# The gate row is spread over the partitions by GpSimd, with two short fillers among TensorE's first transposes

## The chip, the cores and the metric

The kernel runs on one core of a Trainium2 chip. The metric is the device time of one execution in microseconds. A core has five engines that run their own instruction streams in order: TensorE (PE, with its weight loads shown apart as PEld), VectorE (DVE), ScalarE (ACT), GpSimd (POOL) and SyncE (SP, here a queue for DMAs only). They meet through semaphores. PE writes to PSUM (eight banks of 512 fp32 columns), the others work on SBUF, and both memories have 128 partitions.

## The reference

Two branches work on the same x (2048 positions by 512), and a gate mixes them:

```
x = A_x
g = _sigmoid((x * gate_w).sum(-1, keepdims=True))
a = _A_ref(x, A_wqkv, A_wo)
b = _B_ref(x, B_w1, B_b1, B_w2, B_b2)
return g * a + (1 - g) * b
```

Branch a is a local attention: 32 heads of 16, each position attends to 8 positions at distances 0, 2, ... 14, then a product with `wo`. Branch b normalises each row of x, multiplies along the positions with w1 (2048 by 1792), adds b1, takes gelu, and multiplies back with w2, plus b2. The change concerns `gate_w`: the gate's sum for each position needs the 512 numbers of `gate_w` in every partition, since positions lie on the partitions.

## The kernel before

x is held as 16 tiles of 128 positions by 512 (`X`). PE's stream runs in this order: five products on constants (`f_warm`, line 568), transposes of the first four tiles of x (`tx`, line 586) mixed with the first part of branch b on the first four normalised tiles (`lead`, line 618), then the q, k and v projections (line 713), the first product of branch b (`f_ph2`, line 609), in which the two sums of the attention's logits are put (`f_sum`, line 803, called sum0 and sum1), and at the end, tile by tile, the second product of branch b (`f_ph3`, line 937) and the product with `wo` (`f_wo`, line 946). The element-wise products of the attention (q times the shifted k, their sums `qadd`, weights times v) all run on DVE as `tensor_tensor` through the helper of line 468, for two halves of the positions; GpSimd starts DMAs that add or spread parts of them (lines 831, 880, 901).

The program writes each operation with an estimated duration, what it reads and writes, a priority and, in `after`, operations that must have been started. A planner (`_Sched`) runs a list schedule over these estimates when the program is built and so fixes each engine's order; PE's own order is a chain written by hand (`PE`). At run time the order is kept, and an engine waits on the semaphores of what an operation needs. So an operation that comes later than the planner estimated holds up whatever stands behind it on its engine.

The opening, which the change touches, goes like this. For each of the first four tiles t, DVE takes statistics (`stat`, line 623, and `aggr`, line 627), ScalarE makes the reciprocal deviation in two small steps (`rstd`), and DVE normalises the tile (`apply`, line 634) for `lead(t)`. PE transposes the raw tile (`tx(t)`) and an engine copies it from PSUM to `XT` (`ext`, line 598 or 599), which the projections read. The transposed tiles lie in banks 4, 5, 5 and 7 (`TXB`), the transposed biases (`f_tb`, lines 602 and 603) in bank 7; small DVE copies (lines 674 and 675) take them out. The first projections use banks 4 to 7 in turn; those of k on the first 512 positions are called pjk0 to pjk3.

The gate row: ScalarE's queue loads `gate_w` into one partition (line 533) of a tile `GWZ` that GpSimd has set to zero (line 478). A product with a matrix of ones (line 643, `gwbc`) sums over the partitions, so each row of bank 6 holds `gate_w`, and ScalarE copies it to `GWB` (line 656, `evgw`). DVE's 16 gate sums (line 756, z0 to z15) read it. z0 to z5 stand at the head of DVE's stream behind the last normalisation; `rp` (line 679) makes a small indicator matrix for the sums of line 803, and the first q times k product (line 816) follows. GpSimd writes the identity for the transposes (`IDENT`, line 475) right behind two memsets.

Of the kernel before, what the change touches and what calls it, by code (L numbers as in the profile page):

```python
# [5 lines left out]
BF16 = mybir.dt.bfloat16  # L6
# [3 lines left out]
AF = mybir.ActivationFunctionType  # L10
# [3 lines left out]
D = 512  # L14
# [4 lines left out]
NST = S // 128  # L19
NFT = F // 128  # L20
# [8 lines left out]
NLEAD = 4  # L29
AVD = (1, 3, 5, 6)  # L30
GL = 4
# [259 lines left out]
class _Mem:  # L291
# [17 lines left out]
    def view(self, name, dtype, dims, extra=0, p0=0, np_=128):  # L309
        base = self.arena[:].bitcast(dtype)  # L310
        pst = base.ap[0][0]
        esz = mybir.dt.size(dtype)
        o = self.off[name]
        assert o % esz == 0
        return bass.AP(base.tensor, p0 * pst + o // esz + extra, [[pst, np_]] + [list(d) for d in dims])


def bass_gated_mix__sliding_local_dilated__mixer_token_mlp__prompt_kernel(nc, A_x, A_wqkv, A_wo, B_x, B_w1, B_b1, B_w2, B_b2, gate_w, out, dbg=None):
    with contextlib.ExitStack() as es:
# [35 lines left out]
        view = m.view  # L355

        def psub(ap_, p0, np_, offs, dims):
            pst = ap_.ap[0][0]
            return bass.AP(ap_.tensor, ap_.offset + p0 * pst + offs, [[pst, np_]] + [list(d) for d in dims])

        ps = es.enter_context(nc.psum_tensor("ps", [128, 8, 512], FP32))
        esem = {e: es.enter_context(nc.semaphore("sem_" + e)) for e in ("pool", "act", "dve", "pe")}
        sch = _Sched()
        A = sch.add
# [33 lines left out]
        LOG = [view("LOG", BF16, [(UT_, NW), (1, UT_)], extra=h * NW * UT_) for h in range(2)]  # L398
# [12 lines left out]
        E32 = view("E32", FP32, [(1, D)])  # L411
        GWB = view("GWB", BF16, [(1, D)])
        LX = view("LX", BF16, [(D, NLEAD), (1, D)])
        GWZ = view("LOG", BF16, [(1, D)], extra=NLEAD * 128 * GL)
        GW1 = psub(GWZ, 0, 1, 0, [(1, D)])
        JUNK = view("S4", BF16, [(D, 4), (1, D)])
        ZN = view("Z", FP32, [(1, 32)])
        TZ = view("Z", FP32, [(1, 32)], extra=32)
# [2 lines left out]
        IDENT = view("IDENT", BF16, [(1, 128)])  # L421
# [4 lines left out]
        B1R = view("ROWS", BF16, [(1, 128)], np_=NFT)  # L426
        B2R = view("ROWS", BF16, [(1, 128)], extra=128, np_=NST)
        so = [0]

        def small(n, dims=None, extra=0):  # L430
            v_ = view("SMALL", FP32, dims or [(1, n)], extra=so[0] + extra)
            so[0] += n
            return v_
# [20 lines left out]
        B1C = small(NFT)  # L454
        B2C = small(NST)
# [5 lines left out]
        def psb(bank):  # L461
            return ps[:, bank, :].bitcast(BF16)

        def sub(ap_, offs, dims):
            return bass.AP(ap_.tensor, ap_.offset + offs, [list(ap_.ap[0])] + [list(d) for d in dims])
# [4 lines left out]
        def act(o_, i_, f_, **kw):  # L470
            return lambda e: e.activation(out=o_, in_=i_, func=f_, **kw)  # L471
# [3 lines left out]
        A("pool", lambda e: e.affine_select(out=IDENT, in_=ONES, pattern=[[1, 128]], compare_op=ALU.is_equal,  # L475
                                            fill=0.0, base=0, channel_multiplier=-1),
          0.4, reads=["ones"], writes=["ident"], name="ident")
        A("pool", lambda e: e.memset(GWZ, 0.0), 0.4, writes=["gwr"], name="gwz", prio=-50)
        A("pool", lambda e: e.memset(sub(KH[0], 0, [(KR, 4), (1, PAD)]), 0.0), 0.2, writes=["kpad"], name="kpad")  # L479
        A("pool", lambda e: e.memset(sub(V5, 0, [(VR, 4), (1, PAD)]), 0.0), 0.2, writes=["vpad"], name="vpad")  # L480

# [28 lines left out]
        def ld_w(name, tn, d0, d1, res):  # L510
            load(name, WQKV[:, d0:d1, tn * D:(tn + 1) * D], wqkv_v[:, d0:d1, tn * D:(tn + 1) * D], (d1 - d0) * 128 * D * 2, [res])
# [20 lines left out]
        ld_w("wk23", 1, 2, 4, "wk2")  # L532
        load("gw", GW1, bass.AP(gate_w.tensor, gate_w.offset, [[D, 1], [1, D]]), 1024, ["gwr"], issue=0.4, queue="act", order=False)
        load("b1", B1R, B_b1.rearrange("(t p) -> t p", p=128), 4096, ["b1r"], issue=0.4, queue="act", order=False)
# [26 lines left out]
        WONE = nc.const_aps.tensor(1.0, [128, 128], BF16)  # L561
        WROW = nc.const_aps.tensor(1.0, [128, 512], BF16)

        def f_warm(n, bank):
# [4 lines left out]
                return ins  # L569
            return fn  # L570

        chain = [None]

        def PE(fn, dur, reads, writes, name, prio=0):
            op = A("pe", fn, dur, reads=reads, writes=writes, after=([chain[0]] if chain[0] is not None else []), name=name, prio=prio)
            chain[0] = op
            return op
# [12 lines left out]
        def tx(t):  # L590
            PE(f_tx(t), 0.4, ["x%d" % t, "ident"], ["b%d" % TXB[t][0]], "tx%d" % t)

        def ext(t, eng, after):
            bank, o = TXB[t]
            src = sub(psb(bank), o, [(128, 4), (1, 128)])
            dst = sub(XT, t * 128, [(S, 4), (1, 128)])
            if eng == "dve":
                return A("dve", lambda e: e.tensor_copy(out=dst, in_=src), 0.42, reads=["b%d" % bank], writes=["xt0_%d" % t], after=after, name="ext%d" % t, prio=-30)
            return A("act", act(dst, src, AF.Copy), 0.6, reads=["b%d" % bank], writes=["xt0_%d" % t], after=after, name="ext%d" % t, prio=-30)

        def f_tb(e):
            e.transpose(out=psb(7)[:, 512:512 + NFT], in_=B1R, identity=IDENT[0:NFT, 0:NFT])  # L602
            return e.transpose(out=psb(7)[:, 544:544 + NST], in_=B2R, identity=IDENT[0:NST, 0:NST])  # L603

        def f_ph2(ft, bank, s0, s1):
            def fn(e):
# [22 lines left out]
        def rstd(t, after=()):  # L629
            A("act", act(col(SD, t), AG[:, t, 1:2], AF.Ln, bias=1e-5), 0.25, reads=["ag%d" % t], writes=["sd%d" % t], after=after, name="lnl%d" % t, prio=-40)  # L630
            return A("act", act(col(RSTD, t), col(SD, t), AF.Exp, scale=-0.5), 0.25, reads=["sd%d" % t], writes=["rstd%d" % t], name="rs%d" % t, prio=-40)

        def apply(t, after):
            return A("dve", (lambda t_: lambda e: e.tensor_scalar(out=LX[:, t_, :], in0=X[:, t_, :], scalar1=AG[:, t_, 0:1], scalar2=col(RSTD, t_),
                                                                  op0=ALU.subtract, op1=ALU.mult))(t), 0.41, reads=["rstd%d" % t, "st%d" % t, "x%d" % t],
                     writes=["lx%d" % t], after=after, name="ln%d" % t, prio=-40)

        PE(f_warm(5, 0), 2.1, [], ["b0"], "warm0")
        tx(0)
        tx(1)  # L640
        PE(f_tb, 0.2, ["b1r", "b2r", "ident"], ["b7"], "t_b12")
        tx(2)
        PE(lambda e: e.matmul(ps[:, 6, :], lhsT=WONE, rhs=GWZ, start=True, stop=True), 0.4, ["gwr"], ["b6"], "gwbc")  # L643
        def lead(t):
            PE(f_lead(t), 0.87, ["lx%d" % t, "lw%d" % t], ["b%d" % ft for ft in range(GL)], "lead%d" % t)

# [1 line left out]
        ag = aggr(0)  # L648
# [3 lines left out]
        e0 = ext(0, "act", [r0])  # L652
        lead(0)
        ag = aggr(1, [l0])
        r1 = rstd(1)
        ew = A("act", act(GWB, ps[:, 6, :], AF.Copy), 0.6, reads=["b6"], writes=["gwb"], after=[r1], name="evgw", prio=-50)
        tx(3)
        s2 = stat(2, [ag])
        l1 = apply(1, [s2])
        lead(1)  # L660
        ag = aggr(2, [l1])
        r2 = rstd(2)
        s3 = stat(3, [ag])
        l2 = apply(2, [s3])
        ag = aggr(3, [l2])
        e1 = ext(1, "act", [r2, e0])
        r3 = rstd(3, [e1])
        ext(2, "act", [r3])
        e3 = ext(3, "dve", [ag])
        l3 = apply(3, [e3])  # L670
        e3 = l3
        lead(2)
        lead(3)
        A("dve", lambda e: e.tensor_copy(out=B1C, in_=psb(7)[:, 512:512 + NFT]), 0.15, reads=["b7"], writes=["b1c"], after=[e3], name="b1c", prio=-20)
        A("dve", lambda e: e.tensor_copy(out=B2C, in_=psb(7)[:, 544:544 + NST]), 0.15, reads=["b7"], writes=["b2c"], after=[e3], name="b2c", prio=-20)

        def f_rp(e):
            with nc.allow_low_precision(reason="exact 0/1 indicator sums"):
# [53 lines left out]
        for dl in range(4):  # L732
# [3 lines left out]
          reads=["k%d_1" % dl for dl in range(4)], writes=["khalo"], name="khalo")  # L736
# [18 lines left out]
        for t in range(NST):  # L755
            A("dve", (lambda t_: lambda e: e.tensor_tensor_reduce(out=JUNK[:, t_ % 4, :], in0=X[:, t_, :], in1=GWB, scale=1.0, scalar=0.0, op0=ALU.mult, op1=ALU.add,  # L756
                                                                  accum_out=col(Z, t_)))(t), 0.61, reads=["x%d" % t, "gwb", "s4"], writes=["z%d" % t, "jk%d" % (t % 4)], after=[e3],
              name="z%d" % t, prio=-4, delay=1.0 if t in (6, 7) else 0.0)
        A("pool", lambda e: e.memset(ZN, 0.0), 0.15, writes=["zn"], name="zn0")
        A("dve", lambda e: e.tensor_scalar(out=ZN[:, 0:NST], in0=Z, scalar1=ZMAX, scalar2=-1.0, op0=ALU.min, op1=ALU.mult), 0.12,  # L760
          reads=["z%d" % t for t in range(NST)], writes=["zn"], name="zneg", prio=-30)
# [12 lines left out]
        for t in range(NLEAD, NST):  # L774
            A("dve", (lambda t_: lambda e: e.bn_stats(out=ST6[:, t_, :], in_=X[:, t_, :]))(t), 0.6,  # L775
              reads=["x%d" % t], writes=["st%d" % t], after=[e3], name="st%d" % t, prio=-4, delay=1.0 if t in (4, 5, 6, 7) else 0.0)
# [7 lines left out]
          reads=["md"], writes=["vv"], name="ln_var", prio=-20)  # L784
# [3 lines left out]
          reads=["ms", "rstd"], writes=["nmr"], name="ln_nmr", prio=-20)  # L788
        for t in range(NLEAD, NST):
            if t >= NST - LNACT:  # L790
                A("act", act(X[:, t, :], X[:, t, :], AF.Identity, scale=col(RSTD2, t), bias=col(NMR, t)), 0.7, after=[ev2[0][t - NST - 1]], reads=["rstd", "nmr"], writes=["x%d" % t],
                  name="ln%d" % t)
            else:
                A("dve", (lambda t_: lambda e: e.tensor_scalar(out=X[:, t_, :], in0=X[:, t_, :], scalar1=col(MS, t_), scalar2=col(RSTD2, t_),
                                                               op0=ALU.subtract, op1=ALU.mult))(t), 0.33,
                  reads=["rstd", "ms", "st%d" % t], writes=["x%d" % t], name="ln%d" % t, prio=-4)
# [14 lines left out]
        for h in range(2):  # L811
# [43 lines left out]
            if h == 0:  # L855
                A("dve", tt(psub(LOG[0], 0, 32, 0, [(UT_, NW), (1, PAD)]), psub(LOG[0], 0, 32, 0, [(UT_, NW), (1, PAD)]), MASK, ALU.add), 0.2,
                  reads=["mask"], writes=["log0"], name="msk")
# [16 lines left out]
            for c in range(4):  # L874
                for dhi in range(4):
# [5 lines left out]
                                   reads=["att%d" % h], writes=["avw%d_%d_%d" % (h, c, dhi)] + al, after=[prev] if prev else [],  # L881
                                   name="av%d_%d_%d" % (h, c, dhi))
# [10 lines left out]
        for u in range(8):  # L893
# [5 lines left out]
              reads=["avw%d_%d_%d" % (h, c, dhi) for dhi in range(4)] + vr + ["vpad"], writes=PR[b], name="avm%d" % u)  # L899
# [15 lines left out]
        for ft in range(NFT):  # L915
            bank = ft if ft < GL else bank_()
            s0 = NLEAD if ft < GL else 0
            for a_, b_ in ((s0, 8), (8, NST)):
# [3 lines left out]
              reads=["b%d" % bank, "b1c"], writes=["ut%d" % ft] + (["wq", "wq2", "wk", "wk2", "wv"] if ft == 0 else []), name="gel%d" % ft)  # L922
# [69 lines left out]
        for hf, (c0, c1) in enumerate(CH):  # L992
            bank = lastb[hf]
            n_ = c1 - c0
            PE(f_wo(L, bank, c0, c1), 0.87 * n_ / D, ["ot%d" % (L // 2), "wo"], ["b%d" % bank], "wo%d_%d" % (L, hf))
            if hf == 0:
                A("act", act(OUTS[:, NOUT, c0:c1], ps[:, bank, 0:n_], AF.Identity, scale=col(OMG, L), bias=col(C2, L)), 0.4,
                  reads=["b%d" % bank, "omg", "c2"], writes=["outl%d" % hf], name="ev%d_%d" % (L, c0))
# [80 lines left out]
```

## Time and profile before

| what | value |
| --- | --- |
| median of three runs | 163.34 us (163.06 to 163.67) |
| the profiled execution | 162.99 us |
| its span, first to last instruction | 161.7 us |
| granted TensorE clock | 1.0 |
| ScalarE busy | 77.5 us (48%) |
| GpSimd busy | 27.2 us (17%) |
| DMA | 35.54 MB, mean 220 GB/s |
| code transfers (queues q8 and q14, "instruction") | 9 packets, 0.12 MB |

Busy time of an engine in the profile leaves out the issuing of DMAs and semaphore work. The chain of waits is followed back from the last instruction; a time in it is the part of an instruction during which nothing else held up the end. In the timeline, instructions of one form that follow each other are merged, with their number behind an x; so the length of a merged row can hide short gaps. The ends of matmuls are modelled: one of 512 columns shows some 0.38 us but the next starts 0.22 us after it.

### The profile page before, as it was taken

How to read it: one execution, taken by the hardware profiler on the slowest of the kernel's cores; microseconds unless marked ns; L12 is line 12 of the kernel's file. 1: busy time of each engine (PE TensorE's matmuls, PEld its weight loads, DVE VectorE, ACT ScalarE, POOL GpSimd, SP SyncE). 2: the span in 40 equal slices, each digit the busy share in tenths (PEclk: the TensorE clock that was granted, in tenths of full speed). 3: DMA queues.
4: the chain of work that ended last, by engine and by line, in shares of the span. 5: the costliest groups of instructions: out<-in, count | busy, mean ns of one | idle time of the engine just before them, and what ended most of it. 6: DMA issues, size and time to landing. Idle time of an engine off the chain costs nothing.

```text
span 161.7 us, 2009 instructions
## 1 busy us (share of the span) xinstructions
PE 158.7 (98%) x778; PEld 75.9 (47%) x778; DVE 150.9 (93%) x143; ACT 77.5 (48%) x103; POOL 27.2 (17%) x63
## 2 busy tenths in 40 slices
PE   7999999999999999999999999999999999999994
PEld 3455555555554444444444444444444444444652
DVE  2969999999999999999999999999999999999943
ACT  3827666679999381999311344420111111111153
POOL 4000011000000001200792030008580003020000
DMA  4899999999924999999399999999999913949504
GB/s 133 260 228 267 190 295 292 252 212 216 321 92 111 308 292 245 163 296 190 78 321 360 336 298 294 214 311 290 344 206 214 199 50 78 186 109 211 134 32 162
DMA packets 45303, 35.54 MB, mean 220 GB/s; under 512 B 8045, under 2 KB 42094, under 8 KB 45294
## 3 DMA queue, kind: packets, MB, share of 16 engines
q1 hardware_dynamic: 41392, 22.75, 53.4%
q0 software_dynamic: 3696, 12.59, 36.3%
q8 instruction: 6, 0.10, 0.2%
q10 hardware_dynamic: 206, 0.08, 0.2%
q14 instruction: 3, 0.02, 0.0%
HBM read 19.15 MB, written 2.11 MB: 131 GB/s over the span
## 4 chain that ended last, share of the span: by engine, by line
PE 98%; DVE 0%; issue 0%
PE ps L937 30%; PE ps L609 28%; PE ps L713 26%; PE ps L946 9%; PE ps L618 2%; PE ps L568 1%; PE ps L803 1%; PE ps L586 1%; DVE arena L955 0%; PE ps L643 0%; PE ps L602 0%; PE ps L603 0%
## 5 line engine op out<-in xcount | busy, mean ns | idle before, releaser
L468 DVE TENSOR_TENSOR arena<-arena 128x4096 bf16<-128x4096 bf16 (+6 forms) x71 | 125.7, 1807 | 1.5 <-DMA arena<-arena 0.3
L937 PE MATMUL ps<-arena 128*128 128x512 bf16 (+2 forms) x238 | 50.2, 366 | 0.0
L471 ACT ACTIVATE arena<-ps,arena 128x512 bf16<-128x512 f32 (+1 forms) x29 | 20.9, 727 | 55.5 <-PE ps L946 40.6
L609 PE MATMUL ps<-arena 128*128 128x512 bf16 x208 | 45.4, 379 | 0.0
L713 PE MATMUL ps<-arena 128*128 128x512 bf16 x192 | 41.6, 379 | 0.0
L471 ACT ACTIVATE arena<-ps 128x512 bf16<-128x512 f32 (+3 forms) x38 | 31.5, 843 | 14.4 <-PE ps L713 11.2
L937 PEld LDWEIGHTS ps<-arena 128*128 128x128 bf16 x238 | 23.3, 98 | 25.4
L609 PEld LDWEIGHTS ps<-arena 128*128 128x128 bf16 x208 | 20.2, 98 | 24.9 <-issue 0.8
L713 PEld LDWEIGHTS ps<-arena 128*128 128x128 bf16 x192 | 21.7, 113 | 19.7
L880 POOL DMA_DIRECT2D arena<-arena x32 | 17.1, 664 | 23.1 <-DVE arena L468 14.0
L471 ACT ACTIVATE arena<-arena 128x512 bf16<-128x512 bf16 (+6 forms) x27 | 15.2, 565 | 10.1 <-DVE arena L468 9.2
L946 PE MATMUL ps<-arena 128*128 128x512 bf16 (+2 forms) x68 | 15.6, 366 | 0.0
L831 POOL DMA_DIRECT2D arena<-arena x3 | 3.8, 1270 | 62.3 <-DVE arena L468 62.3
L1028 ACT ACT_TABLE_LOAD x9 | 11.5, 1283 | 2.3 <-POOL arena L479 2.2
L756 DVE CUSTOM_DVE_ANT_0 arena<-arena 128x512 bf16<-128x512 bf16 x16 | 10.2, 688 | 1.3 <-DMA arena<-in_A_x_dram 1.3
L901 POOL DMA_DIRECT2D arena<-arena x4 | 4.9, 1226 | 31.4 <-DVE arena L468 31.4
L946 PEld LDWEIGHTS ps<-arena 128*128 128x128 bf16 x68 | 6.6, 98 | 7.2
L775 DVE BATCH_NORM_STATS2 arena<-arena 128x6 f32<-128x512 bf16 x12 | 7.3, 677 | 0.0
L623 DVE BATCH_NORM_STATS2 arena<-arena 128x6 f32<-128x512 bf16 x4 | 2.7, 669 | 2.9 <-DMA arena<-in_A_x_dram 2.9
L955 DVE TENSOR_SCALAR arena<-ps,arena 128x512 bf16<-128x512 f32 (+1 forms) x2 | 1.3, 660 | 3.1 <-PE ps L946 3.0
L618 PE MATMUL ps<-arena 128*128 128x512 bf16 x16 | 4.0, 381 | 0.0
L568 PE MATMUL ps<-const-bfloat16-1.0 128*128 128x512 bf16 x5 | 2.3, 624 | 0.8 <-PEq L1064 0.8
(39 smaller groups left out, 19.0 us busy)
## 6 DMA issues: line engine op xcount, KB each, us to landing
arena<-in_B_w_dram SPq DMA_DIRECT2D x8, 896.0 KB, 13.3
arena<-arena POOLq DMA_DIRECT2D x6, 1024.0 KB, 9.2
arena<-in_B_w_dram SPq DMA_DIRECT2D x5, 1024.0 KB, 8.8
arena<-arena POOLq DMA_DIRECT2D x32, 128.0 KB, 7.3
arena<-arena POOLq DMA_DIRECT2D x1, 2048.0 KB, 17.9
out_dram<-arena SPq DMA_DIRECT2D x15, 128.0 KB, 2.6
arena<-in_B_w_dram SPq DMA_DIRECT2D x2, 768.0 KB, 13.6
arena<-in_A_wqkv_dram SPq DMA_DIRECT2D x4, 256.0 KB, 5.2
```

The source lines that it names most:

```text
L468: return lambda e: e.tensor_tensor(out=o_, in0=a_, in1=b_, op=op_)
L471: return lambda e: e.activation(out=o_, in_=i_, func=f_, **kw)
L609: ins = e.matmul(ps[:, bank, :], lhsT=W1S[W1AT[ft // 2]][:, st, 128 * (ft % 2):128 * (ft % 2) + 128], rhs=(LX if st < NLEAD else X)[:, st, :],
L618: ins = e.matmul(ps[:, ft, :], lhsT=LW[:, t, 128 * ft:128 * ft + 128], rhs=LX[:, t, :], start=(t == 0), stop=False)
L713: ins = e.matmul(ps[:, bank, :], lhsT=sub(WQKV, dt * 3 * D + tn * D + dl, [(4, 128)]), rhs=XT[:, dt, sb * 512:(sb + 1) * 512], start=(dt = ...
L756: A("dve", (lambda t_: lambda e: e.tensor_tensor_reduce(out=JUNK[:, t_ % 4, :], in0=X[:, t_, :], in1=GWB, scale=1.0, scalar=0.0, op0=ALU.m ...
L775: A("dve", (lambda t_: lambda e: e.bn_stats(out=ST6[:, t_, :], in_=X[:, t_, :]))(t), 0.6, reads=["x%d" % t], writes=["st%d" % t], after=[e ...
L880: prev = sch.dma("pool", (lambda d_, s_: lambda e: e.dma_start(d_, s_))(dst, src), 131072, ds, issue=1.0, reads=["att%d" % h], writes=["av ...
L901: sch.dma("pool", (lambda d_, s_: lambda e: e.dma_start(d_, s_, accum_op=ALU.add, max_dma_last_dim=4096))(sub(PB[b], 0, [(2048, 2), (1, 20 ...
L937: ins = e.matmul(ps[:, bank, 0:c1 - c0], lhsT=W2S[i // 2][:, ft, 128 * (i % 2):128 * (i % 2) + 128], rhs=UT[:, ft, c0:c1], start=(ft == 0) ...
L946: ins = e.matmul(ps[:, bank, 0:c1 - c0], lhsT=OT[:, i // 2, dl, 128 * (i % 2):128 * (i % 2) + 128], rhs=WO[:, dl, c0:c1], start=False, sto ...
L1028: e.preload_act_table_set(want)
```

## The change

The gate row is loaded to one partition, without the zeroed tile around it. GpSimd copies partition 0 to all 128 with `partition_broadcast` into `GWB`, and this operation depends on the gate row and on the normalisation of the fourth tile (`l3`). PE's product and ScalarE's copy are gone. The copies of the transposed tiles move: ScalarE takes tiles 1, 2 and 3, each one place earlier in its order than before, and DVE takes none. PE gets two products of 128 columns on constants (`f_fill`, bank 0), one behind the first transposes and one behind those of the biases, and the biases' transposes go to bank 6.

```diff
-        GWZ = view("LOG", BF16, [(1, D)], extra=NLEAD * 128 * GL)
-        GW1 = psub(GWZ, 0, 1, 0, [(1, D)])
+        GW1 = view("LOG", BF16, [(1, D)], extra=NLEAD * 128 * GL, np_=1)
...
-        A("pool", lambda e: e.memset(GWZ, 0.0), 0.4, writes=["gwr"], name="gwz", prio=-50)
...
+        def f_fill(n, bank):
+            return lambda e: e.matmul(ps[:, bank, 0:n], lhsT=WONE, rhs=WROW[:, 0:n], start=True, stop=True)
...
-            e.transpose(out=psb(7)[:, 512:512 + NFT], in_=B1R, identity=IDENT[0:NFT, 0:NFT])
-            return e.transpose(out=psb(7)[:, 544:544 + NST], in_=B2R, identity=IDENT[0:NST, 0:NST])
+            e.transpose(out=psb(6)[:, 512:512 + NFT], in_=B1R, identity=IDENT[0:NFT, 0:NFT])
+            return e.transpose(out=psb(6)[:, 544:544 + NST], in_=B2R, identity=IDENT[0:NST, 0:NST])
...
         tx(0)
+        PE(f_fill(128, 0), 0.1, [], ["b0"], "fill0")
         tx(1)
-        PE(f_tb, 0.2, ["b1r", "b2r", "ident"], ["b7"], "t_b12")
+        PE(f_tb, 0.2, ["b1r", "b2r", "ident"], ["b6"], "t_b12")
+        PE(f_fill(128, 0), 0.1, [], ["b0"], "fill1")
         tx(2)
-        PE(lambda e: e.matmul(ps[:, 6, :], lhsT=WONE, rhs=GWZ, start=True, stop=True), 0.4, ["gwr"], ["b6"], "gwbc")
...
-        ew = A("act", act(GWB, ps[:, 6, :], AF.Copy), 0.6, reads=["b6"], writes=["gwb"], after=[r1], name="evgw", prio=-50)
...
-        r2 = rstd(2)
+        e1 = ext(1, "act", [r1, e0])
+        r2 = rstd(2, [e1])
...
-        e1 = ext(1, "act", [r2, e0])
-        r3 = rstd(3, [e1])
-        ext(2, "act", [r3])
-        e3 = ext(3, "dve", [ag])
-        l3 = apply(3, [e3])
+        e2 = ext(2, "act", [r2])
+        r3 = rstd(3, [e2])
+        ext(3, "act", [r3])
+        l3 = apply(3, [ag])
+        gwp = A("pool", lambda e: e.partition_broadcast(GWB, GW1), 0.5, reads=["gwr"], writes=["gwb"], deps=[l3], name="gwb")
...
-        A("dve", lambda e: e.tensor_copy(out=B1C, in_=psb(7)[:, 512:512 + NFT]), 0.15, reads=["b7"], writes=["b1c"], after=[e3], name="b1c", prio=-20)
-        A("dve", lambda e: e.tensor_copy(out=B2C, in_=psb(7)[:, 544:544 + NST]), 0.15, reads=["b7"], writes=["b2c"], after=[e3], name="b2c", prio=-20)
+        A("dve", lambda e: e.tensor_copy(out=B1C, in_=psb(6)[:, 512:512 + NFT]), 0.15, reads=["b6"], writes=["b1c"], after=[e3], name="b1c", prio=-20)
+        A("dve", lambda e: e.tensor_copy(out=B2C, in_=psb(6)[:, 544:544 + NST]), 0.15, reads=["b6"], writes=["b2c"], after=[e3], name="b2c", prio=-20)
```

## The prediction

> **What bounds the kernel now.** I read the page's first lines and the chain of waits, then the opening 15 us of the timeline, then the two places where TensorE (PE) has to meet a VectorE (DVE) result.
>
> ```profile
> span 161.7 us, 2009 instructions
> ...
> PE 158.7 (98%) x778; PEld 75.9 (47%) x778; DVE 150.9 (93%) x143; ACT 77.5 (48%) x103; POOL 27.2 (17%) x63
> ...
> PE 98%; DVE 0%; issue 0%
> ```
>
> PE is busy for 98% of the span and the chain that ended last never leaves it, so a change is worth what it moves in PE's stream. DVE at 93% is close behind. The chain in order of time (start, length, what):
>
> ```profile
> 4.77 0.22 PE ps L643
> 4.98 0.87 PE ps L618 x4
> ...
> 8.88 41.44 PE ps L713 x192
> 50.32 6.04 PE ps L609 x28
> 56.36 0.98 PE ps L803 x16
> ```
>
> From 8.88 on PE runs without a hole. Line 643 is the product that the change removes: it holds the chain for 0.22 us. Line 803 at 56.36 is the first place where PE must have DVE's sums (sum0 reads what the second `qadd(2, ...)` wrote). The opening, from the timeline (start, length, instruction, in brackets the idle time before it and who ended it):
>
> ```profile
> 0.80 0.53 POOL L478 MEMSET arena<- 128x512 bf16 x1 [0.29 <-POOLq L1064]
> ...
> 1.86 0.28 ACTq L500 DMA_DIRECT2D arena<-in_gate_w_dram  x1
> ...
> 3.55 0.34 PEld L586 LDWEIGHTS ps<-arena 128*128 128x128 bf16 x4 [0.19 <-DMA arena<-in_A_x_dram]
> ...
> 6.83 0.55 PEld L618 LDWEIGHTS ps<-arena 128*128 128x128 bf16 x4 [0.39 <-DVE arena L634]
> ...
> 7.37 0.41 DVE L634 TENSOR_SCALAR arena<-arena 128x512 bf16<-128x512 bf16 x1 [0.20 <-ACT arena L471]
> ...
> 7.84 0.55 PEld L618 LDWEIGHTS ps<-arena 128*128 128x128 bf16 x4 [0.46 <-DVE arena L634]
> 7.86 0.68 DVE L756 CUSTOM_DVE_ANT_0 arena<-arena 128x512 bf16<-128x512 bf16 x1
> ...
> 11.66 0.69 DVE L756 CUSTOM_DVE_ANT_0 arena<-arena 128x512 bf16<-128x512 bf16 x1 [1.27 <-DMA arena<-in_A_x_dram]
> ...
> 14.07 0.28 DVE L679 TENSOR_REDUCE arena<-arena 128x32 bf16<-128x128 bf16 x1
> 14.29 8.90 DVE L468 TENSOR_TENSOR arena<-arena 128x4096 bf16<-128x4096 bf16 x4
> ```
>
> Two things are to be seen. PE waits for DVE's normalised tiles before lead2 (0.39) and lead3 (0.46): until 7.84 PE follows DVE and ScalarE, not its own work. And DVE has one hole, the 1.27 us before 11.66; from 14.29 it runs on to 155.71 (its last run of 16 element-wise instructions starts at 123.82 and lasts 31.89). Where DVE meets sum0, DVE's timeline from 50 to 57 has
>
> ```profile
> 46.52 11.21 DVE L468 TENSOR_TENSOR arena<-arena 128x8192 bf16<-128x8192 bf16 x3
> ```
>
> Those are the two `qadd` (4.42 each by the 8192-column row) and one `qkw` (2.29). The end is 57.73, less 2.29 gives 55.44 for the second `qadd`; PE takes it up at 56.36, so DVE may be 0.9 us late there and no more. The later meetings are wider: sum1 has 1.4 (DVE 94.10 - 4.42 = 89.68 against 91.12), wo12 at the end 1.3 (155.71 against 154.39 + 3 x 0.87 = 156.99).
>
> **What is removed.** The 128x512 memset (0.53, started 0.46 ahead of the next) at GpSimd's head: the identity comes about 0.46 us sooner, but tx0 at 3.04 waits for x0 and not for the identity (written by 1.83), so 0. PE's product, 0.22 on the chain: lead0's weight load had 0.16 idle waiting for DVE anyway, and the 0.39 before lead2 swallows the rest, so 0; were that cover gone, it would be a gain of 0.22. ScalarE's copy of line 656 (0.58): its slot at 5.22 goes to ext1, ext2 takes ext1's at 6.23, and ext3 takes ext2's at 7.24. All three stand where an equal 0.58 copy stood, so rstd2 and rstd3 keep their places and the last transposed tile is still out at 7.82, 0.9 ahead of the projections. ext1 needs tx2 as well (they share bank 5), which is over by 4.9: no wait. DVE's copy ext3 (0.39) goes, yet the next DVE instruction, the last normalisation at 7.37, waited for ScalarE anyway (0.20 idle), so 0.
>
> **What is added on PE.** Two 128-column fillers. The widest such row is four transposes in 0.53, 0.13 each. The first stands in the 0.19 that tx1 waits for x1; the second pushes tx2 by up to 0.13, less than the 0.22 that left. 0; without cover, 0.13 each. The bias transposes move from bank 7 to bank 6: pjk2 rather than pjk3 waits for the two small copies, which end near 7.95, ahead of both.
>
> **What is added on GpSimd, and the wait it makes.** The broadcast waits for the gate row (issued at 1.86; the nearest small load on that queue lands in 2.2: 4.06) and for the last normalisation (7.37 + 0.41 = 7.78). Queued behind its result is DVE's z0, and behind z0, in order, all that DVE does. In GpSimd's own queue the next is the accumulating DMA issued at 23.51, which waits for DVE anyhow. Call T the time at which z0 may start. DVE then has z0 to z3, 7.86 to about 10.31, 2.46; then two statistics and z4, z5, 11.66 to 14.07, 2.41. The `rp` reduction, which waited for nothing but its turn, is taken first while z0 waits. The products at 14.29 can therefore start at T + 4.87, and DVE is late by D = T - 9.42. The x4 hole is used up in this. PE loses D - 0.9.
>
> The broadcast's own length: no row shows one. From below the affine select over 128 columns, 0.29; from above four of these, 1.16; I take 0.53, the 128x512 memset, which writes the same tile. With that alone T = 7.78 + 0.53 = 8.3, D is negative and nothing is lost.
>
> But it is the first time that GpSimd runs this operation: in the trace it does memsets, one affine select and DMA issues. What a first call costs no row shows. From below 0; ScalarE's change of function is a row of that kind (line 1028, 1.28 each), and 1.28 would hide too. From above I take transfers that GpSimd itself starts, since code for its cores must come to it from memory while the weight loads run:
>
> ```profile
> arena<-arena POOLq DMA_DIRECT2D x6, 1024.0 KB, 9.2
> ...
> arena<-arena POOLq DMA_DIRECT2D x32, 128.0 KB, 7.3
> arena<-arena POOLq DMA_DIRECT2D x1, 2048.0 KB, 17.9
> ```
>
> The stretch from 4 to 12 us has the DMA engines at 80 to 90% and more, so a fetch there is not quick: I take 8.25, between the 7.3 and the 9.2, and not 17.9, which is 2 MB. It starts when the queue reaches the broadcast, which I place behind the wait for the gate row and beside the wait for DVE: 4.06. T = 4.06 + 8.25 + 0.53 = 12.84; D = 3.42; PE loses 2.5 at sum0. Sum: 161.7 + 2.5 = 164.2 of span; the profiled execution lies 1.29 above its span (162.99) and the median 0.35 above that: **165.8**.
>
> The Trainium skill (GPSIMD Engine Reference, section 2.1, Instruction dispatch) says that a first call to a freshly loaded kernel costs about 6 us of code load that shows as no instruction in a profile. This trace has nothing to hold against that, since GpSimd's few operations start as soon as their inputs are there. Put in place of 8.25 it would give T = 10.59, D = 1.17 and a loss of 0.3: an estimate of 163.6 us, within 0.5% of the median and so on the side of the first rival below.
>
> **The rivals.**
> *The first call is short or free* (chance 0.25). Place: between 4.06 and 7.78 in GpSimd's queue, price up to 5.8 us; it decides as long as T stays under 10.3 (9.42 + 0.9). For it: the affine select at 1.54 also was a first call, and stands right behind the memset that ended at 1.46. Against it: that operation is in the kernel from its start and may be at hand, a broadcast across partitions is of another kind. Time: all edits at nothing, 163.3.
> *The fetch starts late* (0.10): the queue stands at the DVE wait first, so it begins at 7.78. T = 7.78 + 8.25 + 0.53 = 16.56, D = 7.1, loss 6.2: 169.6. For it: the row L634 that the broadcast waits for is the later of its two inputs. Against: a load needs no input.
> *The fetch stands at the head of the queue* (0.08), ahead of the identity: ready at 1.5 + 8.25 = 9.8. tx0 moves there; from 3.04 to 8.88 PE did 0.7 of transposes ahead of lead0, then 0.87 x 4 and 0.22, so the projections could start at 9.8 + 0.7 + 3.7 = 14.2, 5.3 later: 168.6. Against: nothing in the diff moves the identity.
> *A gain* (0.04): PE's start is earlier by the 0.39 and 0.46 that it idles. It would need DVE's normalisations sooner, and no edit touches their chain: 162.5.
>
> **How the numbers follow.** My forecast has 0.50, with its own range from 164.4 (fetch 6.8) to 167.4 (fetch 9.8); 0.03 is for something else that costs. The measurement can tell 0.5%, 0.8 us, from no change. Slower 0.50 + 0.10 + 0.08 + 0.03 = 0.71; same 0.25; faster 0.04. The range must take in the first rival below and the head-of-queue case above: 163.1 to 168.9; what is left out is the gain and most of the late fetch.
>
> **What would show it.** DVE's first L756 instruction with some 4.5 to 5 us of idle ahead of it, ended by GpSimd, in place of starting at 7.86; `rp` ahead of it; no hole before 11.66's successors; the products of 14.29 at about 17.7; weight loads of L803 at 56.3 + 2.5 with idle ended by DVE L468; PE's projections still at 8.7. If L756 starts at 8.3, the first rival holds. If PE's first transposes are late, the head-of-queue one. My forecast is wrong if the idle is there and sum0 doesn't wait, for then DVE had more slack than I read.

## The result, and the profile after

The changed kernel takes 170.17 us (169.24 to 170.71), the kernel before in the same runs 163.28: a ratio of 1.042 (1.0396 to 1.0443). That is 6.9 us slower, above the forecast's 165.8 and outside its range. The page of the changed kernel, its span, busy times and the chain by engine:

```profile
span 169.1 us, 1994 instructions
...
PE 159.5 (94%) x764; PEld 76.9 (45%) x779; DVE 150.8 (89%) x142; ACT 77.6 (46%) x103; POOL 27.4 (16%) x63
...
PE 93%; issue 5%; DVE 0%; POOL 0%; POOLq 0%
```

The engines do the same work as before; what is new is that 5% of the chain is "issue", time in which an engine waited for nothing that the profile shows. The chain in order of time says where (start, length, what):

```profile
0.79 0.20 POOL arena L473
1.05 7.46 issue
8.51 0.29 POOL arena L474
8.85 0.60 PE ps L587 x4
...
10.78 1.71 PE ps L619 x4
...
12.92 3.29 PE ps L619 x12
16.20 1.73 PE ps L715 x8
```

All of the loss lies ahead of 16.2: the projections (L715 here, L713 before) start at 16.20 and not at 8.88, 7.3 later, and the span is 7.4 longer. GpSimd's affine select (L474), which writes the identity for the transposes, stands still for 7.46 us behind the memset whose output is all that it reads. In the kernel before, the same operation, the first transposes and VectorE's second normalisation stood here (start, length, instruction):

```profile
1.54 0.29 POOL L475 TENSOR_SCALAR_AFFINE_SELECT arena<-arena 128x128 bf16<-128x128 bf16 x1
...
3.04 1.12 PE L586 MATMUL ps<-arena 128*128 128x128 bf16 x8
...
5.35 0.41 DVE L634 TENSOR_SCALAR arena<-arena 128x512 bf16<-128x512 bf16 x1
```

The opening of the changed kernel in the timeline (in brackets the idle time before an instruction and who ended it):

```profile
8.51 0.28 POOL L474 TENSOR_SCALAR_AFFINE_SELECT arena<-arena 128x128 bf16<-128x128 bf16 x1 [7.52 <-issue]
...
8.85 0.60 PE L587 MATMUL ps<-arena 128*128 128x128 bf16 x4 [5.73 <-POOL arena L474]
...
9.49 0.60 ACT L470 ACTIVATE arena<-ps 128x512 bf16<-128x512 bf16 x1 [5.14 <-PE ps L587]
...
10.45 0.41 DVE L635 TENSOR_SCALAR arena<-arena 128x512 bf16<-128x512 bf16 x1 [4.99 <-ACT arena L470]
...
10.58 1.91 PE L619 MATMUL ps<-arena 128*128 128x512 bf16 x4
...
15.68 0.55 POOL L672 PARTITION_BROADCAST arena<-arena  x1 [6.10 <-issue]
...
16.26 0.69 DVE L758 CUSTOM_DVE_ANT_0 arena<-arena 128x512 bf16<-128x512 bf16 x1 [2.71 <-POOL arena L672]
```

TensorE waits for the identity. ScalarE's copy of the first transposed tile waits for TensorE, and since the two small steps for tile 1 stand behind that copy, VectorE's second normalisation comes at 10.45, where it had been at 5.35. The identity had been written at 1.83 and was first used at 3.04, so only 1.2 us of the delay were covered. A second stop of GpSimd, 6.10, is ahead of the broadcast: this is the one that the forecast had in mind. It makes the first gate sum wait 2.71.

### The profile page after: what moved, and what is told of

Same layout as the page of the kernel before. It is cut to its first block, busy times and chain, and to the rows that moved or that the text cites. A ratio compares the mean times of both kernels' runs of the same rounds, so it can differ in the third digit from the quotient of the medians.

```text
span 169.1 us, 1994 instructions
## 1 busy us (share of the span) xinstructions
PE 159.5 (94%) x764; PEld 76.9 (45%) x779; DVE 150.8 (89%) x142; ACT 77.6 (46%) x103; POOL 27.4 (16%) x63
## 4 chain that ended last, share of the span: by engine, by line
PE 93%; issue 5%; DVE 0%; POOL 0%; POOLq 0%
PE ps L939 28%; PE ps L610 26%; PE ps L715 24%; PE ps L948 8%; PE ps L619 3%; PE ps L805 1%; PE ps L587 1%; DVE arena L957 0%; PE ps L571 0%; POOL arena L474 0%; POOL arena L473 0%; PE ps L603 0%; PE ps L604 0%; POOLq L474 0%; POOLq L1066 0%
## 5 line engine op out<-in xcount | busy, mean ns | idle before, releaser
L715 PE MATMUL ps<-arena 128*128 128x512 bf16 x188 | 41.4, 379 | 0.2
L715 PEld LDWEIGHTS ps<-arena 128*128 128x128 bf16 x192 | 21.7, 113 | 19.7
L587 PE MATMUL ps<-arena 128*128 128x128 bf16 x16 | 2.4, 311 | 5.7 <-POOL arena L474 5.7
L635 DVE TENSOR_SCALAR arena<-arena 128x512 bf16<-128x512 bf16 x4 | 1.7, 413 | 5.7 <-ACT arena L470 5.7
```

The lines of the kernel that those rows point to most:

```text
L715: ins = e.matmul(ps[:, bank, :], lhsT=sub(WQKV, dt * 3 * D + tn * D + dl, [(4, 128)]), rhs=XT[:, dt, sb * 512:(sb + 1) * 512], start=(dt = ...
```

## The experiments

Three theories. A: GpSimd holds the code of one set of operations at a time; the affine select and the broadcast are in different sets, and the last one used stays for the next execution, whose first select must then fetch the other back. Such an exchange of sets is called a swap below. B: something else in the opening does it. C: a program that holds a broadcast has its code fetched at the head, each time.

**The unused broadcast at the tail.** The kernel before, and as GpSimd's last operation (`lastp` is the last accumulating DMA):

```diff
...
+        A("pool", lambda e: e.partition_broadcast(ONES, psub(IDENT, 0, 1, 0, [(1, 128)])), 0.5, reads=["ident"], writes=["ones"], after=[lastp], name="tailb")
```

> The kernel before, with one more partition_broadcast at the very end of GpSimd's queue, behind the last accumulating DMA; nobody reads what it writes, so the gate still goes over TensorE and ScalarE. Theory A (GpSimd holds the code of one set of operations at a time; the affine select and the broadcast are in different sets, and whichever ran last stays there for the next execution): the swap at the end is hidden under 15 us of other work, but the next execution's affine select waits some 7.5 us as in the changed kernel, the identity comes at about 9 and the time is 170 to 171. Theory B (the delay comes from what the diff does to the opening: the removed memset, the moved copies, the fillers): 163.3. Theory C (the broadcast's code is fetched once, at the head, in any program that holds a broadcast): 170 as well; the next run tells A from C.

It took 170.55 us on only two runs (170.04 and 171.06), ratio 1.0446 (1.0385 to 1.0506). In its timeline of GpSimd the two ends of the execution are

```profile
8.84 0.28 POOL L475 TENSOR_SCALAR_AFFINE_SELECT arena<-arena 128x128 bf16<-128x128 bf16 x1 [7.38 <-issue]
```

```profile
157.50 1.37 POOL L910 PARTITION_BROADCAST arena<-arena  x1 [5.99 <-issue]
```

An operation 150 us later, whose output nobody reads, costs the whole 7 us, at the head. Theory B falls. Within one execution the tail can't act on the head, so either the set stays over from the execution before (A) or the program's mere contents count (C).

**The other set put back at the tail.** The changed kernel with an explicit load at GpSimd's tail (`load_library` loads a set; `standard` is one that holds the affine select):

```diff
...
+        def f_tail(e):
...
+            e.load_library(library_config.standard)
+            return e.memset(ONES, 1.0)
+        A("pool", f_tail, 0.25, reads=["ident"], writes=["ones"], after=[lastp], name="tailm")
```

> The changed kernel, with a load of the set that holds the affine select put at the end of GpSimd's queue, behind the last accumulating DMA. Theory A: the identity is there at about 1.3 again, the broadcast's own swap starts near 2.1 and takes 6 to 7.5, so the gate row is spread at 8.7 to 10.2; DVE's first gate sum idles 1 to 2.4 us more than before, which the old hole of 1.27 and the 0.9 of slack at sum0 take up: 163.0 to 164.0. Theory C: the fetch at the head stays, 170. My forecast on record, with a swap of 8.25 that starts at 4.06, would give 165.8.

163.34 us, ratio 0.9996 (0.9978 to 1.0015). GpSimd at the head, then at the tail:

```profile
1.30 0.29 POOL L474 TENSOR_SCALAR_AFFINE_SELECT arena<-arena 128x128 bf16<-128x128 bf16 x1 [0.29 <-POOL arena L473]
9.15 0.56 POOL L672 PARTITION_BROADCAST arena<-arena  x1 [6.78 <-DVE arena L681]
```

```profile
152.19 0.20 POOL L915 MEMSET arena<- 128x128 bf16 x1 [6.90 <-issue]
```

The broadcast is still in the program and still pays its swap of 6.8, but the identity is there at 1.6: C falls, A holds. The swap back costs 6.90 at the tail, where it is done at 152 of 161.9. The swap for the broadcast is named after a VectorE instruction, which had ended at 8.24; the wait lasted longer than that. The idle time begins when GpSimd's memsets are through (9.15 - 6.78 = 2.37). That the swap begins there too, and not after the gate row's load, is read from its length: from 4.06, where the prediction puts the gate row, it would have had 5.1 us, and the shortest other swap in these runs took 5.99. The first gate sum started at 9.74, VectorE's products at 14.61 and not 14.29, and sum0 did not notice.

**One set for both.** The set that holds the broadcast holds an affine select as well. In the changed kernel, ahead of the identity:

```diff
...
+        nc.gpsimd.load_library(library_config.all_libraries[1])
```

> The changed kernel, with one explicit load at the head of GpSimd's queue of a set that holds both operations, so that neither asks for another. Theory A: the set stays from one execution to the next, nothing is fetched, the identity is at 1.3 and the gate row is spread at about 8.4: 162.8 to 163.6, which is what all other edits of the change are worth. Theory C: a fetch at the head in each execution, 170.

163.25 us, ratio 1.0000 (0.9982 to 1.0017). GpSimd's timeline:

```profile
1.25 0.29 POOL L477 TENSOR_SCALAR_AFFINE_SELECT arena<-arena 128x128 bf16<-128x128 bf16 x1
7.88 0.54 POOL L675 PARTITION_BROADCAST arena<-arena  x1 [5.57 <-DVE arena L679]
```

No swap in either place, though the same load stands at the head of each execution: a load of what is there already costs 0.2 us at most (GpSimd's first memset starts at 0.97 and not at 0.79), and the time doesn't show it. This run is also the worth of all other edits of the change together: nothing.

**TensorE kept busy.** The changed kernel with `f_warm(26, 0)` in place of `f_warm(5, 0)`:

> The changed kernel, with 26 instead of 5 products on constants ahead of the first transposes, so that TensorE is busy until about 8.5. In the changed kernel the projections start 7.3 us later than before: 5.8 is the wait for the identity (first transpose 8.85 against 3.04), and 1.5 is lost behind it, where the products of line 619 follow each other at 0.43 us and not at 0.22. Theory: that 1.5 is TensorE being slow after 5.7 us without work; kept busy it runs at full pace and the time is 168.3 to 169.0. Rival: the slow stretch comes from its inputs (the normalised tiles and ScalarE's steps are late too), and the time stays at 170.2.

169.72 us, ratio 1.0376 (1.0325 to 1.0426): a miss. The head swap happened to take longer here (8.22 of idle), the first transposes came at 9.55, and yet the projections started at 14.30, 1.7 sooner than in the changed kernel. In the opening behind the transposes

```profile
10.59 1.03 PE L619 MATMUL ps<-arena 128*128 128x512 bf16 x4
```

takes 1.03 where the changed kernel's same line has 1.91. From the first transposes to the projections it took 4.75 us and not 7.2, so here the slow pace was worth 2.4. The pace was thus TensorE's own, but the time did not follow, since something else now came last:

```profile
16.77 0.55 POOL L672 PARTITION_BROADCAST arena<-arena  x1 [6.48 <-issue]
...
17.35 0.69 DVE L758 CUSTOM_DVE_ANT_0 arena<-arena 128x512 bf16<-128x512 bf16 x1 [3.63 <-POOL arena L672]
```

```profile
63.38 1.05 PE L805 MATMUL ps<-arena 128*32 128x512 bf16 x16 [1.43 <-DVE arena L467]
```

The second swap follows the first on GpSimd, so the gate sums start at 17.35, and TensorE waits at the sums (L805) for VectorE. The prediction's account of a late gate row gives this loss: with T, the start of the first gate sum, at 17.35, T - 9.42 - 0.9 is 7.0, and the profiled execution took 170.09 against 162.99, 7.1 more. In the changed kernel T is 16.26, which gives 5.9; that wait was hidden because TensorE was 7.3 late already.

**The same without the second swap.** The tail broadcast (first run) with 26 products:

> The kernel before with the unused broadcast at the tail (e1, 170.55), with 26 products on constants ahead of the first transposes. Here only the identity is late; the gate row goes over TensorE, so no second swap can hold up VectorE as it did in e4. If the part of the loss that lies behind the identity is TensorE's slow pace after its idle time, 0.9 us of e1 (9.18 to 15.76, 6.6, against 3.04 to 8.72, 5.7) go away, up to 1.8 by e4's 4.75: 168.7 to 169.7, and what is left is the wait for the identity alone. Rival: nothing goes away, 170.5.

168.78 us, ratio 1.0367 (1.0311 to 1.0422), 1.8 less than with 5 products (170.55), although the identity came 0.6 later. From the first transposes (9.79) to the projections (14.60) it took 4.8 us, and 6.6 in the first run (9.18 to 15.76). There is no wait at the sums. So the pace of TensorE after 6 us of idle time is worth about 1.8 here. Of this the later identity took 0.6 back: the profiled executions differ by 1.15 (170.04 and 168.89), while the 1.8 between the medians rests on only two runs of the first, 1.0 apart. What is left, 5.5 (168.78 against the 163.31 of before), is the wait for the identity, less what the opening makes up since its other inputs are there.

**The swap for the broadcast made late.** The run with the restored set, where the load waits for the fourth normalised tile:

```diff
+        def f_gwb(e):
...
+            e.load_library(library_config.all_libraries[1])
+            return e.partition_broadcast(GWB, GW1)
-        gwp = A("pool", lambda e: e.partition_broadcast(GWB, GW1), 0.5, reads=["gwr"], writes=["gwb"], deps=[l3], name="gwb")
+        gwp = A("pool", f_gwb, 0.5, reads=["gwr"], writes=["gwb"], deps=[l3], name="gwb")
```

> The run with the restored set (e2), with one thing moved: the load for the broadcast waits for the fourth normalised tile (7.9) in place of starting as soon as GpSimd's queue gets there (2.2). The load is then late by some 5.7 us. If my account of what a late gate row costs is right (products of q and k at T + 4.87, TensorE loses T - 9.42 - 0.9 at sum0), a swap of 6.0 to 7.0 gives T of 14.5 to 15.5 and a loss of 4.2 to 5.2: 167.5 to 168.5, with TensorE's weight loads of the sums waiting for VectorE. Rival: VectorE has other slack, or the planner's order hides it, and the time stays at 163.3 as in e2.

168.61 us, ratio 1.0328 (1.0303 to 1.0353). VectorE, then TensorE:

```profile
15.82 0.69 DVE L762 CUSTOM_DVE_ANT_0 arena<-arena 128x512 bf16<-128x512 bf16 x1 [7.59 <-POOL arena L675]
...
20.69 4.49 DVE L467 TENSOR_TENSOR arena<-arena 128x4096 bf16<-128x4096 bf16 x2
```

```profile
61.85 1.05 PE L809 MATMUL ps<-arena 128*32 128x512 bf16 x16 [1.49 <-DVE arena L467]
```

The swap took 7.4 (7.88 to 15.24, where the broadcast starts), over the 7.0 that I had set as a bound, and the time is 0.1 above my range. T is 15.82 and the products start at 20.69, T + 4.87 to the hundredth. The sums come at 61.85 against 56.29, 5.6 late; T - 9.42 - 0.9 is 5.5, and the time is 5.3 above the 163.31 of before.

**Without the fillers.** The run with one set, less the two `PE(f_fill(128, 0), ...)` lines:

> The run with one set for both operations (e3), without the two fillers. My forecast put them at nothing, since the first stands in a wait for x1 and the second takes the place of the removed product: 163.0 to 163.6, not to be told from e3 (163.25). Rival: the fillers keep TensorE from slowing down in the opening; without them the products of line 618 run at 0.43 for longer and the time is 163.7 to 164.5.

163.25 us, ratio 0.9996 (0.9980 to 1.0011): where the identity comes in time, the fillers are worth nothing either way.

No run beat the kernel before. The best forms of the change (one set, or the set put back) equal it.

## Why the prediction was wrong, and where it was right

**The step that failed** is the one on the first call: "But it is the first time that GpSimd runs this operation". I took the code as one thing to be fetched once, at the broadcast. The traces show an exchange: the broadcast's code goes in and the affine select's goes out, and the next execution pays to have it back. That second half stands in front of the identity, at the very head of the path that sets TensorE's start, where only 1.2 us of the 7.46 were covered. The sum had the identity only as a term of 0, for coming sooner. Worse, I used the row that could have warned me, the affine select right behind its memset, as a sign that first calls may be free; it showed only that its set was still there from the execution before.

**The rival that came nearest in place** was the fetch at the head of the queue, with a chance of 0.08 and 168.6 us, and the sign named for it, late first transposes, is what the trace shows. I set it aside because "nothing in the diff moves the identity": true of the order, and no reason. Its mechanism was also another one (the broadcast's fetch asked for early), and its price was 1.6 short. The fetch is shorter than I took it, 7.46 and not 8.25, so the identity came at 8.8 and not 9.8. But from there to the projections 7.2 us went by (8.85 to 16.04), not 4.4: I priced TensorE at the pace of before and forgot that 5.7 us of idle time come first. Of the 2.8 us that were missing, the changed kernel with 26 products puts 2.4 on that pace (1.8 in the run with the tail broadcast); the other 0.4 was not traced.

**The rival nearest in number** was the fetch that starts late, 169.6, and that is luck. Its T of 16.56 is close to the 16.26 measured, but the swap was late because it follows the one at the head, and not for VectorE's tile; and its loss lay hidden under TensorE's own delay. The late-swap run is this rival's mechanism by itself: 168.61.

**The broadcast's swap** took 6.1 to 7.4 and not 8.25. With the identity in time it started at 2.4 and not 4.06, since the load stands ahead of both waits, and then the loss is nil, as the run with the restored set shows; so this term of the sum, 2.5, should have been 0 for that case. In the changed kernel it started at 9.58, behind the first swap. The sentence from the Trainium skill (GPSIMD Engine Reference, section 2.1, Instruction dispatch), some 6 us that show as no instruction, was nearer than my rows: the swaps measured here are 6.0 to 8.2, and none shows as an instruction. The 163.6 that I worked out with it is what the swap for the broadcast does alone, within the noise (163.34), though that swap starts earlier and lasts longer than in that sum. It has no swap at the head either.

**What held.** The account of a late gate row: T + 4.87 and the slack of 0.9 at sum0, to 0.1 us in the late-swap run. The broadcast's own 0.53 (0.54 to 0.56 measured in the opening). `rp` ahead of the gate sums. And the edits that I put at nothing: the removed product, copy and memset, the moved copies, the moved bank and the fillers come to nothing together, as the run with one set shows. Of these only the fillers were tried alone.

## What to carry to other kernels

A new operation on an engine that runs loaded code isn't priced by its own length: ask which set it belongs to, which other operations of that engine need another, and what the execution leaves behind for the next one, since the price can land at the head of the kernel, far from the edit. If a swap can't be avoided by taking all operations from one set, put the swap back at the tail, under work that runs anyway (6.9 us hidden here), and let the other swap start early (from 2.4 it cost nothing, from 7.9 it cost 5.3). And when a wait in front of an engine is removed, look at what was hidden behind it: the second swap cost nothing until TensorE was faster.

## What the runs showed of the hardware

Swaps at the head of the execution cost 7.4 to 8.2 us, those in the middle or at the tail 6.0 to 7.4. Sorted by direction, those back to the affine select's set cost 6.9 to 8.2 and those to the broadcast's 6.0 to 7.4. Why they differ was not tried. They leave no instruction in the trace: only idle time ended by "issue", or put down to a releaser that had been done before. Nor do the DMA queues show them: q8 and q14, for code, have 9 packets and 0.12 MB in the changed kernel as in the one before. What fills the 6 to 8 us is thus not seen; that it is a set being loaded is read from the runs with explicit loads.

After 5.7 us without work TensorE ran its 512-column products at 0.43 us each (1.71 for four in the chain) where it had taken 0.22, while the granted clock in the records stayed at 1.00. Counted from the first transposes, the slow stretch lasted 5.4 us there (8.85 to about 14.3) and 4.0 in the run with the tail broadcast (9.18 to about 13.2). Gaps of 0.8 and 1.3 us, ahead of the transposes in the two runs with 26 products, left the pace at 0.22. The windows of the changed kernel (stretch and its length; busy us and instructions of PE, PEld, DVE, ACT and POOL; clock; DMA share; GB/s) show the clock:

```profile
2.00:9.00 7.00, 1.27 (x5) 0.30 (x4) 2.46 (x6) 1.69 (x3) 0.49 (x7) 1.00 0.89 256
9.00:16.00 7.00, 7.00 (x36) 3.76 (x35) 2.35 (x9) 3.27 (x10) 0.90 (x15) 1.00 1.12 233
```

The clock column (1.00) is the same in both, so the slow pace must be read from the spacing of the products. The Trainium skill (TensorE: Matmul & The Clock Gate, Part 1) has TensorE at half its rate after some 3.4 us of idle time until it has been busy for about as long. The spacing here agrees with the half rate; the slow stretches were longer, 4.0 and 5.4.
